# A fused attention, gated convolution and mixer kernel: four transfers placed behind the square weights, attention pieces at other places, low parts on VectorE

## The chip, the cores and the metric

The kernel runs on one core of one Trainium2 chip. The metric is the device time of one execution in microseconds (us). TensorE (PE in the rows; PEld is its weight load) multiplies, VectorE (DVE), ScalarE (ACT) and GpSimd (POOL) do the rest, and SyncE (SP; SPq is its queue) issues every transfer of the kernel. Each engine takes its instructions strictly in order, so an instruction that waits holds back all that stand behind it on its engine.

## The reference, cut to what matters

Four batches of 576 positions, 8 heads of 64. Attention is the sum of a global one on sequences averaged by 4 and a local one over a band of 7; a gated convolution layer and a mixer layer follow, each of plain float32 matmuls.

```python
def attention(q, k, v):          # (4, 8, 576, 64) each
    out_d = softmax(scale * mean4(q) @ mean4(k).T) @ mean4(v)
    out_local = softmax(where(abs(i - j) < 4, scale * q @ k.T, -1e9)) @ v
    return repeat4(out_d) + out_local

def moe(x):                      # x: (4, 576, 512)
    gate = sigmoid(causal_conv5(x, conv_w))
    return gate * (x @ w_val) @ w_out

def moe2(x):
    u = x + (relu(x.T @ w_tok1) @ w_tok2).T
    return u + relu(u @ w_ch1) @ w_ch2
```

## The kernel before

Precision is kept by splitting each float32 operand into a high part (ScalarE copies it to the type that TensorE takes (fp32r in the rows), line 718 in `hi_lo`) and a low part (the operand less its high part, line 719, on VectorE or GpSimd). Each product is then three matmuls (`mm3`, lines 284 to 286). The weights come as 64-bit words whose bits VectorE joins to float32 in three instructions (lines 153, 155, 158, `join_bits`; two fetched chunks at a time, so six instructions), then ScalarE and VectorE split them.

**Stages.** `start` (line 506) does the attention of the first batch: its order on TensorE, ScalarE, VectorE and SyncE is written out by hand in the table ORDER (line 81). In it `wf` fetches a chunk of the two square weights w_val and w_out (16 chunks, `w_fetch`, line 662), `wp` joins two chunks (`w_join`), `xf` adds the local output to `x_f` (line 637), `xh` and `xl` make the high and low part of `x_f` (lines 655 and 658), `g` and `ka` to `kd` are the taps of the convolution (lines 640 and 646). Chunks are joined in the order of the table WORD; the seventh join (`wp6`) takes chunks 9 and 11, the eighth (`wp7`) 13 and 15, all of w_out.

Then a generator `first_products` walks the four batches: `p1` (the products with w_val, called p_val; with w_out, called p_x; the token mixing r_ps and p_h) and `c1` (g_ps, the first channel product). Beside it, `mix` advances the attention of batches 1 to 3 (`attention`, line 338, cut in 26 pieces per batch by its yields) whenever the running estimate of the main stream passes the next number of the table AT (line 64). Two equal numbers let two pieces run right behind each other. Only TensorE's order is fixed by that; the other engines' instructions are put in order by a scheduler when the program is built. `c2` and `ch2_new` do the last channel product.

**Pieces of one head pair** (four per batch): `sums` (line 348; the averaged q and k on VectorE, the tile qk_d; the averaged v in two additions v_sb and vd, lines 358 and 359, on GpSimd for batches 1 and 2 and on VectorE for batch 3), `low_scores` (sc_d), `low_turn` (pt_d), `loc_scores` (sc_l), `low_out` (o_d), `loc_turn` (pt_l), `loc_out` (o_l).

**Buffers that tie the steps.** The tile for v in four parts (`load_v4`, line 300, tag v4) has one buffer (NV4 = 1): the load of a head pair's v waits until the sums of the pair before it (vd, line 359) are done. The fetched weight chunks share three buffers (NWD = 3): a fetch waits for the join of the chunk three before it. Both kinds of load stand in SyncE's one queue.

**The loads of batch 1** are put into SyncE's order behind the first batch's last v load (`begun`, line 489) for the first two head pairs; for the later two nothing holds them:

```python
if i + 1 < NHP:
    with behind(begun, i + 1):
        hpd[i + 1] = load(b, i + 1)
```

Of the kernel before, what the change touches and what calls it, by code (L numbers as in the profile page):

```python
# [46 lines left out]
MM = 0.133  # L47
FILL = {3: 1, 5: 1, 12: 1, 14: 1, 17: 1, 20: 1, 24: 1, 25: 2, 27: 1, 31: 2}
PRIME = 20, 24
# [14 lines left out]
AT = {  # L64
# [10 lines left out]
}  # L75
# [17 lines left out]
def kernel(ctx, tc, qk, vw, v4, w_val, conv_w, w_out, w_tok1, w_tok2, w_ch1, w_ch2, out):  # L93
# [40 lines left out]
    def flush():  # L134
        while pending:
            with behind_pace():
                pending.pop(0)()

    def fetch_bits(src, n, rows, shape=None):
        x = T(sb, [128, n, 2], I32, "w64", NWD, name="w64")[0:rows]  # L140
        if shape is None:
            nc.sync.dma_start(out=x, in_=src.bitcast(I32).rearrange("p (n t) -> p n t", t=2))
        else:
            nc.sync.dma_start(out=x.rearrange("p (k n) t -> p k n t", k=shape[0]),
                              in_=src.bitcast(I32).rearrange("p k (n t) -> p k n t", t=2))
        return x
# [191 lines left out]
    def attention(b):  # L338
# [9 lines left out]
        def sums(hp):  # L348
            d = hpd[hp]
            w = d.pop("v4")  # L350
            qk_d = T(sb, [128, 2, SD], F32, "qkd", ND, name="qk_d")
            qd, kd = qk_d[:, 0], qk_d[:, 1]
            qk_4 = d["qk"][:, :, 3:3 + S].rearrange("p i (a r) -> p i a r", r=4)
            nc.vector.tensor_reduce(out=qk_d, in_=qk_4, axis=AX.X, op=ALU.add)
            d["qkd"] = qd, kd
            vd = T(sb, [72, 2, 128], F32, "vd", NVD, name="vd")
            eng = nc.vector if b in (3,) else nc.gpsimd
            eng.tensor_tensor(out=w[:, 0:2], in0=w[:, 0:2], in1=w[:, 2:4], op=ALU.add)
            eng.tensor_tensor(out=vd, in0=w[:, 0], in1=w[:, 1], op=ALU.add)
            d["vd"] = [vd]  # L360
# [117 lines left out]
        for i in range(NHP + 1):  # L478
# [27 lines left out]
    def start():  # L506
# [218 lines left out]
    def hv(hs):  # L725
        return slice(hs * HS, hs * HS + HS)
# [11 lines left out]
    def p1(b):  # L738
# [88 lines left out]
        for hs in range(2):  # L827
            us.append(pair("u", "uhl", NUH))
            for c in range(KC):
# [258 lines left out]
```

## Time and profile before

| | |
|---|---|
| median of 3 runs | 615.67 us (612.16 to 616.51) |
| the profiled execution | 616.48 us; its span 614.6 us |
| busy over the span | PE 575.1 (94%), PEld 530.1 (86%), DVE 449.8 (73%), ACT 336.9 (55%), POOL 111.8 (18%) |
| GpSimd's additions and products | low parts (lines 659, 719), sums (358, 359), scaling of the exponentials (336) |
| bytes moved | 127.56 MB, mean 208 GB/s |

The 1.8 us between span and time lie outside the profile. From 225 us on TensorE is busy for 97% or more of the time; what it lacks is nearly all in the first 180 us, where the profile's slices show VectorE at nine tenths and more. So the page as a whole says "TensorE bound", and the early stages have to be read one by one.

### The profile page before, as it was taken

To read this page: it belongs to the slowest core of one execution; us is meant where nothing else is said; L and a number is where in the kernel's file an instruction comes from. 1 tells how busy PE (TensorE), PEld (TensorE's weight loads), DVE (VectorE), ACT (ScalarE), POOL (GpSimd) and SP (SyncE) were. 2 spreads that over 40 slices of the span, in tenths; PEclk is the share of its full clock that TensorE was granted. 3 is DMA by queue.
4 is the path that set the end of the run, shared out by engine and by line. 5 is a ranking of instruction groups with operands and counts; after the bars stand their busy time and mean duration, and the time that the engine had idled before them with its cause. 6 is when DMAs were issued, how large, how long until landed. Compare 5 with 4: busy or idle time off the path is not lost.

```text
span 614.6 us, 13154 instructions
## 1 busy us (share of the span) xinstructions
PE 575.1 (94%) x4975; PEld 530.1 (86%) x4975; DVE 449.8 (73%) x1019; ACT 336.9 (55%) x1118; POOL 111.8 (18%) x112
## 2 busy tenths in 40 slices
PE   8883769898999999999999999999999999999997
PEld 4772758677989889998988999999999999999997
DVE  6996987897977777762665549378975777677684
ACT  4983566566567566356635644435443645544642
POOL 1064303254102224214411410200000000000000
PEclk9877978999999999999999999999999999999999
DMA  8762144265873468794464799163977997968702
GB/s 282 243 182 88 41 137 144 67 230 190 291 245 127 144 206 261 264 307 144 144 201 149 227 309 327 34 231 142 331 259 246 351 340 236 352 212 278 260 2 77
DMA packets 84287, 127.56 MB, mean 208 GB/s; under 512 B 6720, under 2 KB 67008, under 8 KB 84224
## 3 DMA queue, kind: packets, MB, share of 16 engines
q1 hardware_dynamic: 84224, 126.72, 62.4%
q8 instruction: 39, 0.64, 0.4%
q14 instruction: 24, 0.20, 0.1%
HBM read 85.76 MB, written 40.94 MB: 206 GB/s over the span
## 4 chain that ended last, share of the span: by engine, by line
PE 61%; DVE 17%; ACT 9%; DMA 8%; issue 2%; POOL 2%; SPq 1%; DVEq 0%; ACTq 0%; POOLq 0%
PE p_o L285 6%; PE p_o L286 6%; PE p_o L284 6%; PE g_ps L284 6%; PE g_ps L285 6%; PE g_ps L286 6%; DMA qk_sb<-in_qk_dram 3%; DVE gate_sb L459 2%; PE p_x L284 2%; PE sc_l L417 2%; PE p_val L284 2%; PE p_val L285 2%; DMA v_sb<-in_v_dram 2%; PE p_val L286 2%; ACT e_l L331 2%
## 5 line engine op out<-in xcount | busy, mean ns | idle before, releaser
L284 PE MATMUL g_ps<-u_hl,w_hl 128*128 128x288 f32 x384 | 116.3, 303 | 0.3 <-ACT w_hl L168 0.3
L286 PE MATMUL g_ps<-u_hl,w_hl 128*128 128x288 f32 x384 | 113.5, 296 | 0.6 <-DVE w_hl L169 0.6
L285 PE MATMUL g_ps<-u_hl,w_hl 128*128 128x288 f32 x384 | 113.4, 295 | 0.5 <-POOL u_hl L719 0.5
L718 ACT ACTIVATE g_hl<-r_back 128x384 fp32r<-128x384 f32 x126 | 65.5, 525 | 59.5 <-PE p_o L286 53.9
L719 DVE TENSOR_TENSOR g_hl<-r_back,g_hl 128x384 fp32r<-128x384 f32 x126 | 67.7, 554 | 31.0 <-ACT g_hl L718 29.8
L285 PE MATMUL p_o<-g_hl,ch_w 128*128 128x384 f32 x252 | 85.0, 337 | 1.0 <-DVE g_hl L719 0.6
L286 PE MATMUL p_o<-g_hl,ch_w 128*128 128x384 f32 x252 | 84.7, 336 | 0.0
L284 PE MATMUL p_o<-g_hl,ch_w 128*128 128x384 f32 x252 | 84.6, 336 | 0.0
L901 ACT ACTIVATE r_sb<-g_ps 128x288 f32<-128x288 f32 x96 | 39.6, 413 | 71.7 <-PE g_ps L286 65.9
L284 PEld LDWEIGHTS g_ps<-u_hl,w_hl 128*128 128x128 f32 x384 | 72.1, 188 | 3.8 <-issue 2.1
L286 PEld LDWEIGHTS g_ps<-u_hl,w_hl 128*128 128x128 f32 x384 | 72.2, 188 | 1.2 <-DVE w_hl L169 1.2
L285 PEld LDWEIGHTS g_ps<-u_hl,w_hl 128*128 128x128 f32 x384 | 72.2, 188 | 1.0 <-POOL u_hl L719 0.8
L849 DVE TENSOR_TENSOR r_sb<-r_sb 128x288 f32<-128x288 f32 x84 | 38.2, 468 | 24.9 <-ACT r_sb L901 24.5
L284 PE MATMUL p_val<-x_hl,val_hi 128*128 128x288 f32 x128 | 41.1, 321 | 11.6 <-DVE x_f L637 10.2
L285 PEld LDWEIGHTS p_o<-g_hl,ch_w 128*128 128x128 f32 x252 | 47.3, 188 | 2.4 <-DVE g_hl L719 2.3
L284 PEld LDWEIGHTS p_o<-g_hl,ch_w 128*128 128x128 f32 x252 | 47.3, 188 | 0.0
L286 PEld LDWEIGHTS p_o<-g_hl,ch_w 128*128 128x128 f32 x252 | 47.3, 188 | 0.0
L459 DVE SCALAR_TENSOR_TENSOR gate_sb<-x_f,cw,gate_sb 128x575 f32<-128x575 f32 (+3 forms) x48 | 43.6, 908 | 0.3
L284 PE MATMUL p_x<-y_hl,out_hi 128*128 128x288 f32 x128 | 39.6, 309 | 1.0 <-ACT u_sb L770 0.9
L285 PE MATMUL p_val<-x_hl,val_hi 128*128 128x288 f32 x128 | 39.5, 308 | 0.0
L286 PE MATMUL p_x<-y_hl,out_lo 128*128 128x288 f32 x128 | 38.1, 298 | 1.3 <-DVE out_lo L674 1.3
L286 PE MATMUL p_val<-x_hl,val_lo 128*128 128x288 f32 x128 | 39.1, 306 | 0.0
(154 smaller groups left out, 1338.2 us busy)
## 6 DMA issues: line engine op xcount, KB each, us to landing
r_back<-r_dr SPq DMA_DIRECT2D x21, 1152.0 KB, 10.9
r_dr<-r_sb SPq DMA_DIRECT2D x21, 1008.0 KB, 5.6
w_hl<-w_dr SPq DMA_DIRECT2D x27, 512.0 KB, 5.8
w<-in_w_ch_dram SPq DMA_DIRECT2D x48, 256.0 KB, 3.6
qk_sb<-in_qk_dram SPq DMA_DIRECT2D x16, 589.0 KB, 3.8
w_dr<-w_hl SPq DMA_DIRECT2D x12, 512.0 KB, 3.9
v_sb<-in_vw_dram SPq DMA_DIRECT2D x16, 320.0 KB, 4.4
v_sb<-in_v_dram SPq DMA_DIRECT2D x16, 288.0 KB
```

The costliest lines, as they stand in the source:

```text
L284: nc.tensor.matmul(out_ap, lhsT=lh, rhs=rh, start=first, stop=False)
L285: nc.tensor.matmul(out_ap, lhsT=lh, rhs=rl, start=False, stop=False)
L286: nc.tensor.matmul(out_ap, lhsT=ll, rhs=rh, start=False, stop=last)
L331: nc.scalar.activation(out=e[:, o, :], in_=p[:, c, :], func=AF.Exp, scale=scale, bias=mx[:, o:o + 1], accum_out=sm[:, o:o + 1])
L417: nc.tensor.matmul(p[r0:r0 + 64, c, :], lhsT=qk[r0:r0 + 64, 0, 3 + o:3 + o + WIN], rhs=qk[r0:r0 + 64, 1, o:o + WIN], start=False, stop=(c ...
L459: nc.vector.scalar_tensor_tensor(out=g[:, sh:], in0=x[:, 0:S - sh], scalar=cw[:, hp, k:k + 1], in1=g[:, sh:], op0=ALU.mult, op1=ALU.add)
L718: nc.scalar.activation(out=hi_ap, in_=src_ap, func=AF.Copy)
L719: lo_eng.tensor_tensor(out=lo_ap, in0=src_ap, in1=hi_ap.bitcast(F32), op=ALU.subtract)
L849: nc.vector.tensor_tensor(out=r[:, o], in0=r[:, x], in1=r[:, y], op=op)
L901: paced[0] = nc.scalar.activation(out=r[:, (0, 3, 1, 2)[2 * (i % 2) + hs]], in_=p[:, 0:HS], func=AF.Relu)
```

## The change

Six edits. (1) The loads of batch 1 for its third and fourth head pair are put behind `last_sq`, the fetch of the last chunk of the square weights. (2) The loads of the second head pair keep the old rule. (3) The sums of v of batch 2 go from GpSimd to VectorE. (4) Low parts go from GpSimd to VectorE: of `x_f` for the first three head pairs of the first batch, of x in batch 3, of u in batch 1. (5) ORDER has some steps elsewhere; AT has other numbers, some of them equal. (6) One filling block of `c1` goes one place later (FILL 20 to 21).

```diff
-FILL = {3: 1, 5: 1, 12: 1, 14: 1, 17: 1, 20: 1, 24: 1, 25: 2, 27: 1, 31: 2}
+FILL = {3: 1, 5: 1, 12: 1, 14: 1, 17: 1, 21: 1, 24: 1, 25: 2, 27: 1, 31: 2}
...
-    "a1": "9.96 11.62 13.28 14.95 16.62 18.28 19.94 23.44 25.1 26.77 28.43 30.1 31.19 32.86 34.52 36.18 39.96 "
+    "a1": "9.06 11.62 13.28 14.95 16.62 18.28 21.69 21.69 25.1 26.77 28.43 30.1 31.19 32.11 34.52 36.18 39.96 "
...
-wf10 wf12 Od1 cd2 xf0 wh6 wh7 wl6 elb2 wl7 D3 Tl1 md3 xh0 g0 xl0 L3 ql2 rl2 ed3 ka0 wp4 wf14 wf9 cl1 up1 Ol1 qd3
+wf10 Od1 cd2 xf0 wh6 wf12 wh7 wl6 elb2 wl7 D3 Tl1 g0 md3 xh0 xl0 L3 ql2 rl2 ed3 ka0 wp4 wf14 wf9 cl1 up1 qd3 ml3
...
+    last_fetch = [None]
...
-            nc.sync.dma_start(out=x, in_=src.bitcast(I32).rearrange("p (n t) -> p n t", t=2))
+            last_fetch[0] = nc.sync.dma_start(out=x, in_=src.bitcast(I32).rearrange("p (n t) -> p n t", t=2))
...
-            eng = nc.vector if b in (3,) else nc.gpsimd
+            eng = nc.vector if b in (2, 3) else nc.gpsimd
...
-                with behind(begun, i + 1):
+                with behind(begun, i + 1) if i == 0 else tc.issue_after(last_sq[0].ins) if b == 1 else nullcontext():
                     hpd[i + 1] = load(b, i + 1)
...
-            last_split[0] = (nc.vector if h == NHP - 1 else nc.gpsimd).tensor_tensor(
+            last_split[0] = nc.vector.tensor_tensor(
...
             t["w", c] = fetch_bits(chunks[c][0], WB, 128)
+            last_sq[0] = last_fetch[0]
...
-                hi_lo(xf[b][k][:, hv(hs)], x[0][:, k], x[1][:, k], nc.vector if b in (1,) else nc.gpsimd)
+                hi_lo(xf[b][k][:, hv(hs)], x[0][:, k], x[1][:, k], nc.vector if b in (1, 3) else nc.gpsimd)
...
-                hi_lo(uu, us[hs][0][:, c], us[hs][1][:, c], nc.vector if b in (3,) else nc.gpsimd)
+                hi_lo(uu, us[hs][0][:, c], us[hs][1][:, c], nc.vector if b in (1, 3) else nc.gpsimd)
```

**Place A, SyncE's queue near the end of the first batch's attention.** The names w64 are chunks of the square weights (in_w_out) and then of the token weights (in_w_tok1); v4_sb_1206 is the v of batch 1's second head pair, v4_sb_1367 (1387 after) that of its third. Before:

```order
L142 DMA w64_618<-in_w_out_dram 128x512
L142 DMA w64_620<-in_w_out_dram 128x512
L303 DMA v4_sb_1206<-in_v4_dram 72x1024
L312 DMA v_sb_1213<-in_vw_dram 128x640
L303 DMA v4_sb_1367<-in_v4_dram 72x1024
L142 DMA w64_757<-in_w_out_dram 128x512
L142 DMA w64_759<-in_w_out_dram 128x512
L142 DMA w64_845<-in_w_out_dram 128x512
L142 DMA w64_946<-in_w_tok1_dram 128x512
```

After:

```order
L305 DMA v4_sb_1206<-in_v4_dram 72x1024
L144 DMA w64_618<-in_w_out_dram 128x512
L144 DMA w64_620<-in_w_out_dram 128x512
L314 DMA v_sb_1213<-in_vw_dram 128x640
L144 DMA w64_757<-in_w_out_dram 128x512
L144 DMA w64_759<-in_w_out_dram 128x512
L144 DMA w64_845<-in_w_out_dram 128x512
L144 DMA w64_946<-in_w_tok1_dram 128x512
L305 DMA v4_sb_1387<-in_v4_dram 72x1024
```

The third pair's v went from ahead of three square chunks to behind them and one token chunk; the second pair's v went from behind two square chunks to ahead of them.

**Place B, VectorE where the first batch's attention ends and p_val begins.** x_f_100 is the last of the four x_f tiles, x_hl its parts, qk_d the averaged q and k of batch 1's first head pair, y a product p_val times its gate. Before:

```order
L646 SCALAR_TENSOR_TENSOR gate_sb<-x_f_100,cw,gate_sb 128x287
L659 TENSOR_TENSOR x_hl<-x_f_100,x_hl 128x288
L646 SCALAR_TENSOR_TENSOR gate_sb<-x_f_100,cw,gate_sb 128x286
L646 SCALAR_TENSOR_TENSOR gate_sb<-x_f_99,cw,gate_sb 128x572
L646 SCALAR_TENSOR_TENSOR gate_sb<-x_f_100,cw,gate_sb 128x285
L674 TENSOR_TENSOR out_lo<-wa,out_hi 128x256
L757 TENSOR_TENSOR y_906<-p_val,gate_sb 128x288
```

After:

```order
L648 SCALAR_TENSOR_TENSOR gate_sb<-x_f_100,cw,gate_sb 128x287
L648 SCALAR_TENSOR_TENSOR gate_sb<-x_f_99,cw,gate_sb 128x572
L661 TENSOR_TENSOR x_hl<-x_f_100,x_hl 128x288
L648 SCALAR_TENSOR_TENSOR gate_sb<-x_f_100,cw,gate_sb 128x286
L356 TENSOR_REDUCE qk_d<-qk_sb 128x288
L760 TENSOR_TENSOR y_906<-p_val,gate_sb 128x288
```

The reduction qk_d now stands ahead of the first y; before, it stood behind the joins of two token chunks.

**Place C, VectorE around the maxima of the first low scores of batch 1** (mx from sc_d; w_1014 and w_1048 are token chunks). Before:

```order
L354 TENSOR_REDUCE qk_d<-qk_sb 128x288
L153 TENSOR_SCALAR wa<-w_1014 128x256
L153 TENSOR_SCALAR wa<-w_1048 64x256
L155 SCALAR_TENSOR_TENSOR wa<-w_1014,wa 128x256
L155 SCALAR_TENSOR_TENSOR wa<-w_1048,wa 64x256
L158 SCALAR_TENSOR_TENSOR wa<-w_1014,wa 128x256
L158 SCALAR_TENSOR_TENSOR wa<-w_1048,wa 64x256
L169 TENSOR_TENSOR tok_lo<-wa,tok_hi 128x256 x2
L325 TENSOR_REDUCE mx<-sc_d 72x2 x2
```

After:

```order
L327 TENSOR_REDUCE mx<-sc_d 72x2
L171 TENSOR_TENSOR tok_lo<-wa,tok_hi 128x256
L155 TENSOR_SCALAR wa<-w_1014 128x256
L327 TENSOR_REDUCE mx<-sc_d 72x2
L157 SCALAR_TENSOR_TENSOR wa<-w_1014,wa 128x256
```

Six of the weight instructions that stood ahead of the second maximum now stand behind it.

## Rows read from the trace of the kernel before

**Rows 1.** Stretches: span, then busy time (instructions) per engine, TensorE's clock, DMA share, GB/s

```profile
50.00:60.00 10.00, 1.15 (x5) 1.15 (x6) 4.54 (x9) 1.53 (x5) 3.58 (x4) 0.64 0.32 106
60.00:84.00 24.00, 18.70 (x113) 17.55 (x113) 22.09 (x52) 13.56 (x33) 5.30 (x4) 0.80 0.23 75
84.00:110.00 26.00, 21.76 (x242) 19.01 (x241) 19.03 (x51) 16.50 (x81) 7.04 (x6) 0.93 0.41 133
110.00:140.00 30.00, 27.54 (x278) 22.09 (x279) 29.37 (x60) 19.02 (x74) 12.64 (x12) 1.00 0.45 152
140.00:180.00 40.00, 36.54 (x341) 33.43 (x343) 34.79 (x86) 25.09 (x80) 8.44 (x7) 1.00 0.77 258
```

**Rows 2.** TensorE's waits: total us, times, longest us

```profile
PE p_val L284 <- DVE x_f L637: 10.2, 1, 10.2
PE sc_d L369 <- DVE qk_d L354: 3.5, 1, 3.5
PE sc_l L411 <- DVE wa L155: 1.4, 1, 1.4
PE p_x L286 <- DVE out_lo L674: 1.3, 1, 1.3
```

**Rows 3.** SyncE's queue in order of time: start us, us, what

```profile
38.26 0.33 SPq L303 DMA_DIRECT2D v_sb<-in_v_dram  x1
...
51.63 0.33 SPq L303 DMA_DIRECT2D v_sb<-in_v_dram  x1
52.01 6.44 SPq L142 DMA_DIRECT2D w<-in_w_out_dram  x3
```

**Rows 4.** GpSimd in order of time: start us, us, what, idle before and its releaser

```profile
35.77 1.26 POOL L358 TENSOR_TENSOR v_sb<-v_sb 72x512 f32<-72x512 f32 x1 [2.37 <-issue]
...
39.19 6.25 POOL L659 TENSOR_TENSOR x_hl<-x_f,x_hl 128x288 fp32r<-128x288 f32 x1 [0.96 <-ACT x_hl L656]
45.40 5.41 POOL L358 TENSOR_TENSOR v_sb<-v_sb 72x512 f32<-72x512 f32 x1
50.89 0.72 POOL L359 TENSOR_TENSOR vd<-v_sb 72x256 f32<-72x256 f32 x1
...
67.99 5.30 POOL L719 TENSOR_TENSOR x_hl<-x_f,x_hl 128x288 fp32r<-128x288 f32 x4 [10.85 <-ACT x_hl L718]
```

**Rows 5.** VectorE in order of time, 42 to 82 us

```profile
42.98 0.75 DVE L158 SCALAR_TENSOR_TENSOR wa<-w,wa 128x256 int32<-128x256 int32 x2
43.65 0.81 DVE L646 SCALAR_TENSOR_TENSOR gate_sb<-x_f,cw,gate_sb 128x575 f32<-128x575 f32 x1
...
49.41 0.28 DVE L153 TENSOR_SCALAR wa<-w 128x256 int32<-128x256 int32 x1
55.46 1.04 DVE L153 TENSOR_SCALAR wa<-w 128x256 int32<-128x256 int32 x1 [5.76 <-DMA w<-in_w_out_dram]
...
58.35 0.81 DVE L637 TENSOR_TENSOR x_f<-o_l,x_f 128x290 f32<-128x290 f32 x2
...
60.24 0.45 DVE L659 TENSOR_TENSOR x_hl<-x_f,x_hl 128x288 fp32r<-128x288 f32 x1
60.61 1.66 DVE L646 SCALAR_TENSOR_TENSOR gate_sb<-x_f,cw,gate_sb 128x286 f32<-128x286 f32 x3
...
64.25 0.46 DVE L757 TENSOR_TENSOR y<-p_val,gate_sb 128x288 f32<-128x288 f32 x1 [1.28 <-PE p_val L286]
...
71.57 1.07 DVE L646 SCALAR_TENSOR_TENSOR gate_sb<-x_f,cw,gate_sb 128x288 f32<-128x288 f32 x1
...
73.49 0.51 DVE L646 SCALAR_TENSOR_TENSOR gate_sb<-x_f,cw,gate_sb 128x288 f32<-128x288 f32 x1
...
77.35 1.34 DVE L354 TENSOR_REDUCE qk_d<-qk_sb 128x288 f32<-128x1152 f32 x1
...
81.23 0.81 DVE L325 TENSOR_REDUCE mx<-sc_d 72x2 f32<-72x288 f32 x2
```

**Rows 6.** ScalarE in order of time: the first x_f's tap

```profile
31.88 0.76 ACT L640 ACTIVATE gate_sb<-x_f,cw 128x576 f32<-128x576 f32 x1
```

**Rows 7.** VectorE's groups of one form: busy us, mean ns, idle before

```profile
L358 DVE TENSOR_TENSOR v_sb<-v_sb 72x512 f32<-72x512 f32 x4 | 3.7, 931 | 1.9 <-DMA v_sb<-in_v_dram 1.9
L359 DVE TENSOR_TENSOR vd<-v_sb 72x256 f32<-72x256 f32 x4 | 1.7, 432 | 2.6 <-PE o_d L397 2.6
```

More of the change, by code (lines that the diff above doesn't have):

```diff
@@ L81 @@
 ORDER = """
-qk0 wf0 wf1 qk1 wf2 qk2 va0 vw0 z12 S0 L0 wp0 cwf wf3 qk3 va1 vw1 D0 z14 ml0 wh1 wh0 S1 ela0 md0 wl0 ed0 wl1 S2
-elb0 D1 qd0 rd0 md1 Td0 cwj L1 ed1 ql0 wp1 wf4 wf5 va2 vw2 wf6 cd0 rl0 wh3 D2 wh2 ml1 Tl0 wl3 ela1 Od0 qd1 S3
-rd1 cl0 md2 elb1 Td1 wp2 wf7 va3 vw3 wf8 ed2 L2 ql1 wl2 rl1 cd1 qd2 up0 rd2 Ol0 wh5 ml2 wh4 wl5 ela2 wl4 Td2 wp3
-wf10 wf12 Od1 cd2 xf0 wh6 wh7 wl6 elb2 wl7 D3 Tl1 md3 xh0 g0 xl0 L3 ql2 rl2 ed3 ka0 wp4 wf14 wf9 cl1 up1 Ol1 qd3
-ml3 wh8 wh10 kb0 Od2 ela3 xf1 kc0 xh1 rd3 elb3 xl1 Tl2 kd0 z4 cl2 wl10 ql3 wl8 up2 rl3 Td3 g1 Ol2 wp5 wf11 wf13
-cd3 Od3 ka1 wh12 wh14 wl12 xf2 kb1 xh2 g2 Tl3 xl2 wl14 kc1 up3 z5 ka2 cl3 kd1 Ol3 kb2 wp6 wf15 xf3 wh11 wh9 kc2
-g3 xh3 ka3 gh xl3 kb3 kd2 kc3 wl9 kd3 na sga wl11 wp7 nb wh15 wh13 nc wl13 nd sgb wl15
+qk0 wf1 wf0 qk1 wf2 qk2 va0 vw0 z12 S0 L0 wp0 cwf wf3 qk3 va1 D0 z14 ml0 wh1 wh0 S1 ela0 md0 vw1 wl0 ed0 wl1 D1
+S2 elb0 qd0 rd0 md1 Td0 cwj L1 ed1 ql0 wp1 wf4 wf5 va2 vw2 wf6 cd0 D2 rl0 wh3 wh2 ml1 Tl0 wl3 ela1 Od0 qd1 S3
+vw3 rd1 cl0 md2 elb1 Td1 wp2 wf7 va3 wf8 ed2 L2 ql1 wl2 rl1 cd1 qd2 rd2 Ol0 up0 wh5 ml2 wh4 wl5 ela2 wl4 Td2 wp3
+wf10 Od1 cd2 xf0 wh6 wf12 wh7 wl6 elb2 wl7 D3 Tl1 g0 md3 xh0 xl0 L3 ql2 rl2 ed3 ka0 wp4 wf14 wf9 cl1 up1 qd3 ml3
+wh8 wh10 Ol1 kb0 Od2 ela3 xf1 kc0 xh1 rd3 elb3 xl1 Tl2 kd0 z4 cl2 wl10 ql3 wl8 up2 g1 rl3 Td3 Ol2 wp5 wf11 wf13
+cd3 Od3 ka1 wh12 wh14 wl12 xf2 kb1 xh2 xl2 g2 Tl3 kc1 wl14 up3 z5 ka2 cl3 kd1 Ol3 kb2 wp6 wf15 xf3 wh11 wh9 kc2
+g3 xh3 ka3 gh kd2 xl3 kb3 kc3 wl9 kd3 na sga wl11 wp7 nb wh15 wh13 nc wl13 nd sgb wl15
 """
@@ L289 @@
     xf, gate = {}, {}
-    last_gate, last_copy, last_pe, last_load, last_split = {}, [None], [None], [None], [None]
+    last_gate, last_copy, last_pe, last_load, last_split, last_sq = {}, [None], [None], [None], [None], [None]
     LU = [(0, 6), (6, 10)]
```

14 rows, old and new, of the table AT are left out of this document.

## The prediction, made before the changed kernel ran

> **What bounds the kernel now.** I read three views, in this order. The stretches first [rows 1]: from 50 to 60 us TensorE is busy 1.15 us of 10 and VectorE 4.54, so there everybody waits; from 60 to 84 us VectorE is busy 22.09 of 24 and TensorE 18.70; from 110 to 140 us VectorE has 0.63 us free, TensorE 2.46. The first 140 us are thus set by VectorE or by what VectorE waits for; later TensorE is the bound. TensorE's waits next [rows 2]: two are large, 10.2 us for x_f ahead of the first p_val and 3.5 us for qk_d ahead of the first sc_d; 1.4 and 1.3 us of the same stage follow. Then the engines in order of time, to see what x_f waited for.
>
> The 10.2 us go back like this. VectorE takes the first half of the seventh join at 49.41, then stands still for 5.76 us until a w_out chunk lands [rows 5]. That chunk is one of the three fetches that start at 52.01 [rows 3], so it landed 55.46 - 0.03 - 52.01 = 3.4 us after its issue. Its buffer had been free since the sixth join, whose first last instruction ended at about 42.98 + 0.34 = 43.3 (two take 43.65 - 42.98 = 0.67) [rows 5]. It was issued late because SyncE stood at a v load from 38.6 to 51.63 [rows 3]; and that load waited for GpSimd's vd, which ends at 50.89 + 0.72 = 51.61 [rows 4]. GpSimd was late since its low part of x_f took 6.25 us and its addition v_sb 5.41, where the same addition took 1.26 earlier [rows 4]. Both lie in a stretch in which VectorE ran without a gap; the second ends 1.1 us after VectorE's last instruction (49.41 + 0.28 = 49.69). So GpSimd got hardly anything done as long as VectorE was busy.
>
> **The change, part by part.** *SyncE's order (place A).* The chunk w64_757 no longer stands behind the third pair's v. It goes out when its buffer is free, at the sixth join. That join is later by the low parts that VectorE now makes itself: one costs 60.61 - 60.24 = 0.37 us [rows 5]. The first of them also waits, because ScalarE now makes the tap of 0.76 us [rows 6] ahead of the high part; I take 0.75 us for this one in all (bounds 0.37 and 1.13). So the sixth join is 0.75 + 0.37 = 1.1 us later, the buffer free at 44.4, the chunk there at 44.4 + 3.4 = 47.8. VectorE wants it at 49.41 + 0.20 + 0.75 + 2 x 0.37 = 51.1. The wait of 5.76 us goes, with 3.3 us to spare.
>
> From 49.41 to x_f (58.35) VectorE took 8.94 us: 5.76 waiting; the rest 3.18, of which the join's six instructions need 2 x 0.20 + 4 x 0.335 = 1.74 undisturbed, and 1.4 is disturbance by GpSimd's two instructions there (a join step took 1.04 instead of 0.28 [rows 5]). After: x_f starts at 49.41 + 1.74 + 1.49 = 52.65, which is 5.7 us earlier, and p_val with it, at about 53.15 instead of 58.85.
>
> *VectorE from there to the maxima (places B and C).* Before: 58.35 to 81.23 + 0.81 = 82.0, that is 23.65 us, with one idle time of 1.28 [rows 5]. After, the same instructions stand there but for six that moved behind the second maximum: 0.20 + 4 x 0.335 + 0.335 = 1.9 us less. qk_d (1.34 us) only changes its place, so TensorE's wait of 3.5 us goes without any work being saved. Idle I put at 0.3 instead of 1.28: qk_d and a tap of batch 0 fill the time in which p_val is made. The third pair's v now is summed in this stage instead of before it: 0.6 us of disturbance more. Four GpSimd low parts disturb as before: a tap took 1.07 instead of 0.51 beside them [rows 5], 0.56 for each, 2.3 in all [rows 4]. Sum: 23.65 - 1.9 - 1.0 + 0.6 = 21.4. The maxima end at 52.65 + 21.4 = 74.05: **8.0 us earlier**. I read the gain there and not at p_val: sc_l waits for the exponentials behind these maxima [rows 2], so TensorE, earlier still after p_x, will wait there longer than its 1.4 us.
>
> *Whether 8.0 us reach the end.* The six postponed instructions (1.9 us) have to be made later. VectorE has 26 - 19.03 = 7 us free from 84 to 110 us and 40 - 34.79 = 5.2 from 140 to 180 [rows 1]; these cover them. If that cover is gone they cost 1.9.
>
> *Low parts and sums on VectorE.* Low parts: 3 + 8 + 8 = 19, of 0.37 us each, 7.0 us; sums of batch 2: four times 0.93 + 0.43 [rows 7], 5.4 us. Together 12.4 us, of which 1.5 are in the walk above. Against it: each such GpSimd instruction held VectorE up by between 0 and 0.56 us, with 27 of them gone 0 to 15 us. I take nothing for the rest: 10.9 us are near the middle of what is saved. The bounds are 10.9 lost, and some 4 won. The 8 low parts of batch 3 stand beyond 225 us, where VectorE has room. The sums of batch 2 also wait on VectorE for transfers and for o_d, as those of batch 3 do (1.9 and 2.6 us) [rows 7]; behind a waiting one stand the next joins and y.
>
> VectorE seems too full for more work, and the Trainium skill says so too: the page Perfetto Trace Analysis, Optimizing Scalar/DVE Operations, has it that a saturated VectorE is a reason to give work to ScalarE or even GpSimd. This change does the reverse. Going by that sentence the 12.4 us would be a loss; the rows show that the work on GpSimd costs VectorE time as well, and the same section warns that moving work between those two might not help.
>
> *AT, FILL.* No instruction of TensorE is added. In batch 1 o_d and pt_l follow each other behind the first three quarters of a p_x block. I take zero, bounds 1.5 either way: that is one of the waits of TensorE left in [rows 2].
>
> **Sum.** The profiled execution: 616.48 - 8.0 = 608.5. It is 0.81 above the median of 615.67, to which I hold: 615.67 - 8.0 = **607.7 us**.
>
> **The rivals.** *The wait moves.* v4_sb_1206 now stands ahead of w64_618 and w64_620 (place A) and waits for GpSimd's first vd. If GpSimd is shut out there as it was from 39.19 on (6.25 + 5.41 instead of 1.26 and about 1), chunk 618 goes out at about 42.4, lands at 45.8, and VectorE, at its join at about 43, waits 3 us. Gain 5.0: 610.7. Against it: v4_sb_1038, which feeds that sum, stands two chunks earlier in the queue, and the sum at 35.77 ran freely.
>
> *VectorE gives part of it back.* From 110 to 180 us it has 0.63 + 5.2 = 5.8 us free [rows 1]. Work of 1.9, of 5.4 and, to 250 us, of 8 x 0.37 = 3.0 comes, 10.3 in all; if no disturbance is saved, 4.5 us are on the path: 612.2.
>
> *More is gained.* TensorE's granted clock is 0.64 from 50 to 60 us, 0.80 to 84 us and 0.93 to 110 us [rows 1], so 7.2, 9.6 and 3.6 us at its lower level, each time about a wait. If the stretch that goes with the wait for qk_d (half of the 9.6) is at the upper level, TensorE does the work of 4.8 us in 2.4, and where it is the bound the gain is 10.4; with 1.5 from the pieces' new places 11.9: 603.8.
>
> *Slower.* VectorE saturated from 60 to 250 us, every added instruction on the path: 615.67 - 5.7 + 12.4 = 622.4. It decides when disturbance saves less than about 6 us and VectorE's free time cannot be used because TensorE's fixed order makes it wait at other times. The rule on saturated engines above would have it so. Against it: 7 + 5.2 us free [rows 1].
>
> *Nothing happens:* chunk 757 is late for another reason (its join or the DMA engines), 615.7. Against it: the free buffer at 43.3 and a DMA share of 0.32 [rows 1].
>
> **The numbers.** Forecast 0.56 (604.5 to 611), more gained 0.18, moved wait 0.09, given back 0.08, nothing 0.04, slower 0.05. A measurement of this kernel can tell about 1% from no change, 6.2 us, so below 609.5 is faster, above 621.8 slower. Four fifths of the forecast lie below 609.5, with all of "more": 0.63 faster, 0.05 slower, 0.32 within. The range reaches from 602, beyond "more gained", to 613.5, beyond "given back"; it leaves out "nothing", "slower" and a tenth at the edges. Its lower end is what would come if both large waits went in full, 615.67 - 13.7.
>
> **What would show it.** VectorE has no wait for a w_out chunk at the seventh join; p_val begins at 52.5 to 54.5 us; no wait of sc_d for qk_d; the first maxima end at 73 to 76; sc_l waits longer than before, for ScalarE's exponentials. SyncE does not stand for GpSimd between 38 and 52 us. At 225 us the lead is still 8 us. Wrong: VectorE waits for w64_618 at about 43 us; the lead at 140 us is 8 and at 250 us 4; or v_sb and vd of batch 2 show waits on VectorE that TensorE then has too.

## The result, and the profile after

The changed kernel takes 609.25 us (median of 10 runs, 606.22 to 612.17), beside 614.48 us for the kernel before (10 runs, 611.38 to 617.54): a ratio of 0.990, with a 95% interval from 0.987 to 0.993. The ratio is reckoned from the single executions; the medians alone give 0.9915, a gain of 5.2 us instead of about 6. Forecast were 607.7 us, from 602.0 to 613.5, a gain of 8.0 reckoned from 615.67. The profiled execution took 612.17 us, with a span of 610.4 us; that of before 616.48, with 614.6. Executions of one kernel spread by half a per cent either way, so a difference of 2 or 3 us between two profiles is no finding by itself. Line numbers of the changed kernel are 2 or 3 higher than those of before.

The stretches after, in the columns of [rows 1]:

```profile
50.00:60.00 10.00, 8.05 (x78) 5.64 (x74) 10.00 (x20) 6.05 (x14) 0.00 (x0) 0.83 0.26 84
60.00:84.00 24.00, 18.49 (x149) 16.38 (x148) 23.05 (x58) 13.88 (x45) 5.78 (x6) 0.93 0.31 100
84.00:110.00 26.00, 23.35 (x211) 19.72 (x210) 18.46 (x47) 14.45 (x67) 5.87 (x5) 0.87 0.37 111
110.00:140.00 30.00, 27.43 (x282) 22.34 (x282) 28.73 (x60) 19.83 (x82) 13.04 (x12) 1.00 0.56 188
140.00:180.00 40.00, 38.23 (x383) 35.55 (x382) 35.43 (x87) 27.30 (x97) 2.44 (x2) 1.00 0.76 250
```

From 50 to 60 us VectorE no longer stands still, and TensorE is busy 8.05 us instead of 1.15. In the last stretch TensorE is busy 38.23 us of 40 instead of 36.54. From 84 to 110 us it is busy longer than before (23.35 us against 21.76) with fewer matmuls (211 against 242), at a granted clock of 0.87 instead of 0.93.

TensorE's waits after, as in [rows 2] (the four largest, and the one for x_f):

```profile
PE sc_l L413 <- ACT e_d L333: 6.0, 4, 3.0
PE pt_d L593 <- ACT pts_l L609: 3.3, 1, 3.3
PE p_x L287 <- DVE y_hl L722: 2.3, 1, 2.3
PE sc_d L537 <- DVE x_f L639: 1.8, 1, 1.8
...
PE p_val L286 <- DVE x_f L639: 1.0, 1, 1.0
```

The wait of p_val for x_f is down from 10.2 us to 1.0, that of 3.5 us for qk_d is gone; sc_l waits longer, and p_x and pt_d wait where they did not.

SyncE's queue, GpSimd and VectorE after, in order of time (start us, us, what), as in [rows 3 to 5]:

```profile
46.79 8.21 SPq L144 DMA_DIRECT2D w<-in_w_out_dram  x3
55.10 0.37 SPq L144 DMA_DIRECT2D w<-in_w_tok_dram  x1
55.57 0.35 SPq L305 DMA_DIRECT2D v_sb<-in_v_dram  x1
```

```profile
38.77 1.27 POOL L360 TENSOR_TENSOR v_sb<-v_sb 72x512 f32<-72x512 f32 x1 [3.29 <-DMA v_sb<-in_v_dram]
40.12 1.12 POOL L361 TENSOR_TENSOR vd<-v_sb 72x256 f32<-72x256 f32 x1
```

```profile
28.96 0.29 DVE L155 TENSOR_SCALAR wa<-w 128x256 int32<-128x256 int32 x1 [0.96 <-DMA w<-in_w_val_dram]
...
33.50 1.41 DVE L661 TENSOR_TENSOR x_hl<-x_f,x_hl 128x288 fp32r<-128x288 f32 x1 [0.77 <-ACT x_hl L658]
...
45.28 0.48 DVE L155 TENSOR_SCALAR wa<-w 128x256 int32<-128x256 int32 x2
...
53.16 0.48 DVE L155 TENSOR_SCALAR wa<-w 128x256 int32<-128x256 int32 x2
...
54.90 0.81 DVE L639 TENSOR_TENSOR x_f<-o_l,x_f 128x290 f32<-128x290 f32 x2
...
75.50 0.45 DVE L327 TENSOR_REDUCE mx<-sc_d 72x2 f32<-72x288 f32 x1
```

The seventh join (53.16) runs without a wait, its w_out chunks having been issued from 46.79 on. The addition that took 5.41 us takes 1.27, and vd ends at 41.24 instead of 51.61. The second maximum ends at 75.50 + 0.45 = 75.95 instead of 82.0.

### The profile page after: what moved, and what is told of

It reads as the page before. It is cut to its first block, busy times and chain, and to the rows that moved or that the text cites. A ratio compares the mean times of both kernels' runs of the same rounds, so it can differ in the third digit from the quotient of the medians.

```text
span 610.4 us, 13163 instructions
## 1 busy us (share of the span) xinstructions
PE 578.0 (95%) x4975; PEld 530.7 (87%) x4975; DVE 454.4 (74%) x1046; ACT 336.5 (55%) x1118; POOL 73.5 (12%) x85
## 4 chain that ended last, share of the span: by engine, by line
PE 58%; DVE 21%; DMA 10%; ACT 9%; issue 2%; POOL 0%; SPq 0%; ACTq 0%; DVEq 0%; POOLq 0%
PE p_o L287 6%; PE p_o L288 6%; PE p_o L286 6%; PE g_ps L286 6%; PE g_ps L287 5%; PE g_ps L288 5%; DMA w<-in_w_ch_dram 2%; DVE gate_sb L648 2%; PE p_x L286 2%; PE sc_l L419 2%; DVE gate_sb L461 2%; ACT e_l L333 2%; DMA w<-in_w_val_dram 2%; DVE wa L157 2%; DMA qk_sb<-in_qk_dram 2%; PE p_val L286 2%
## 5 line engine op out<-in xcount | busy, mean ns | idle before, releaser
L461 DVE SCALAR_TENSOR_TENSOR gate_sb<-x_f,cw,gate_sb 128x575 f32<-128x575 f32 (+3 forms) x48 | 40.9, 852 | 0.2
L287 PE MATMUL p_x<-y_hl,out_hi 128*128 128x288 f32 x128 | 38.0, 297 | 2.3 <-DVE y_hl L722 2.3
L286 PE MATMUL p_x<-y_hl,out_hi 128*128 128x288 f32 x128 | 39.3, 307 | 0.5
```

Of the source, the lines that this page charges most:

```text
L286: nc.tensor.matmul(out_ap, lhsT=lh, rhs=rh, start=first, stop=False)
L287: nc.tensor.matmul(out_ap, lhsT=lh, rhs=rl, start=False, stop=False)
L461: nc.vector.scalar_tensor_tensor(out=g[:, sh:], in0=x[:, 0:S - sh], scalar=cw[:, hp, k:k + 1], in1=g[:, sh:], op0=ALU.mult, op1=ALU.add)
```

## The experiments

The table has each kernel's median, the median of before that it stands against, and the ratio with its 95% interval. A ratio of 0.990 is about 6 us. Distances from the changed kernel are reckoned from 0.990; by the medians (0.9915) each gap to a slower kernel is 0.9 us smaller.

| kernel | us | before | ratio |
|---|---|---|---|
| changed kernel | 609.25 | 614.48 | 0.990 (0.987 to 0.993) |
| before + hold of the third pair's v load | 613.34 | 614.91 | 0.9968 (0.9941 to 0.9996) |
| before + first batch's low parts on VectorE | 615.23 | 614.91 | 1.0004 (0.9973 to 1.0036) |
| before + new list | 614.19 | 615.37 | 0.9993 (0.9964 to 1.0023) |
| before + sums of batch 2 on VectorE + AT, FILL | 612.53 | 615.63 | 0.9957 (0.9929 to 0.9985) |
| changed − hold | 610.92 | 614.91 | 0.9934 (0.9904 to 0.9964) |
| changed − first batch's low parts | 611.16 | 614.91 | 0.9938 (0.9906 to 0.9970) |
| changed − new list | 610.83 | 615.37 | 0.9928 (0.9899 to 0.9957) |
| changed − AT, FILL | 612.04 | 615.37 | 0.9952 (0.9923 to 0.9981) |
| changed − sums of batch 2 | 613.06 | 615.56 | 0.9962 (0.9935 to 0.9989) |
| changed − sums of batch 2, x of batch 3, u of batch 1 | 614.59 | 615.37 | 0.9988 (0.9963 to 1.0012) |
| changed + two repairs of the list | 608.45 | 615.56 | 0.9896 (0.9852 to 0.9940) |
| changed + x and u of batch 0 on VectorE | 617.19 | 615.56 | 1.0023 (0.9994 to 1.0052) |

### The wait at the seventh join

Theory 1 is the prediction's: the v load's place in SyncE's queue is the cause of the wait. Theory 2: GpSimd is the cause, which gets nothing done beside VectorE; with the low parts taken off it the load would be free in time, and the hold is not needed. Each was tried alone and taken out of the changed kernel.

The hold alone, on the kernel before (with the bookkeeping of last_sq that it needs):

```diff
-                with behind(begun, i + 1):
+                with behind(begun, i + 1) if i == 0 else tc.issue_after(last_sq[0].ins) if b == 1 else nullcontext():
                     hpd[i + 1] = load(b, i + 1)
```

> The kernel before with one part of the change: the v load of the third pair is held until the last square-weight fetch has been issued, so that it stands behind the three w_out fetches of the seventh join in SyncE's queue. Low parts, order list, times and sums stay those of before. Theory 1 (the queue position of the v load is the cause): the wait of 5.76 us at the seventh join goes, p_val begins 5 to 6 us earlier, the time is about 609. Theory 2 (the cause is GpSimd, which gets nothing done while VectorE is busy): the wait goes too, but the third low part of x_f, which p_val needs, still stands on GpSimd behind its 5.4 us addition; p_val is earlier by 0 to 3 us only, the time 612 to 615.

The wait is gone (seventh join at 51.41 without a gap) and p_val begins at 53.66 instead of 58.85. The time falls by 0.3%, about 2 us (interval 0.2 to 3.6). So p_val does what Theory 1 says, and the time does not: it lies where Theory 2 had it, for another reason than Theory 2 gave.

The low parts alone, on the kernel before:

```diff
-            last_split[0] = (nc.vector if h == NHP - 1 else nc.gpsimd).tensor_tensor(
+            last_split[0] = nc.vector.tensor_tensor(
```

> The kernel before with one part of the change: the first two low parts of x_f of the first batch are made on VectorE instead of GpSimd, as the third was already or now is too; the v load of the third pair stays ahead of the w_out fetches in SyncE's queue. Theory 1: the v load still waits for GpSimd's vd, and the fetches behind it with it; VectorE's wait at the seventh join stays over 3 us and the gain is under 2 us, so 613 or more. Theory 2: GpSimd, free of the low parts, ends vd at about 41 to 43 us instead of 51.6, the v load no longer stands in the way, and the wait goes without any change to the queue: about 609.

The wait shrinks to 0.41 us, p_val begins at 55.24, and the time stays (1.0004). Theory 2 is right about the wait; again nothing reaches the end.

The changed kernel without the hold, and with the first batch's low parts back on GpSimd (the two diffs above, reversed; the edit moves three low parts, not two as the expectations have it):

> The changed kernel without the hold: the v load of the third pair goes back to its old place ahead of the three w_out fetches of the seventh join; all else as changed. Theory 1: SyncE stands at that load again, the seventh join waits, 4 to 6 us are lost against the changed kernel: 613 to 615. Theory 2: in the changed kernel vd of the second pair ends at 41.24 us, so that the load would stand at most until then, while the buffer of the fetch behind it comes free only at 46.8: the hold is worth nothing, 609 within 1.

> The changed kernel with the first two low parts of x_f of the first batch back on GpSimd; the hold and all else as changed. Theory 1: since the fetches no longer stand behind the v load, the wait at the seventh join does not come back, and the time is 609 to 611. Theory 2: GpSimd is shut out again while VectorE is busy (an instruction of about 1 us takes 5 to 6), x_f's low parts come late and p_val, which needs them, with them: 2 to 5 us lost, 611 to 614.

In neither does the seventh join wait (53.25 and 53.52, no gap). They come out 0.34% and 0.38% above the changed kernel, some 2 us each, which the intervals don't separate from nothing. The wait of Theory 1 does not come back, as Theory 2 said; the low parts may be worth the 2 us of Theory 2's lower end.

### The list, and what the wait is worth

Since both single parts took the wait away and gained 0 to 2 us, the rest had to carry the 6 us. First the list:

```diff
 ORDER = """
-(list of before)
+(list of after)
```

> The kernel before with one part of the change: the new ORDER list for the first stage (first batch) and nothing else: no hold, low parts and sums on GpSimd, the old times AT and FILL. The two single parts tried before took the wait at the seventh join away (5.76 us before, 0.0 with the hold alone, 0.5 with the low parts alone), and p_val began 5.2 and 3.6 us earlier, yet the time fell by 1.6 us and not at all. Theory 3: most of what the change gains comes from the new list (fewer and shorter waits of TensorE between 60 and 100 us, since qk_d and two taps no longer stand ahead of the maxima): 610 to 611. Theory 1 and 2 (the removed wait): the list alone gives nothing, 614 to 615.

> The changed kernel with the ORDER list of before; hold, low parts, sums, AT and FILL as changed. The counterpart of the run with the new list alone. Theory 3 (the list carries it): 612 to 614, about as with the hold alone. Theory 1 and 2 (the wait carries it, with both parts together): 609 to 610.

The new list alone gives nothing measurable (0.9993); without it the changed kernel still gains 0.72%. Theory 3 falls. The profile with the list alone shows something else. Here the v load stands ahead of the w_out chunks and GpSimd makes the low parts, both as before. GpSimd and VectorE there, in order of time:

```profile
38.09 1.86 POOL L358 TENSOR_TENSOR v_sb<-v_sb 72x512 f32<-72x512 f32 x1 [2.35 <-DMA v_sb<-in_v_dram]
40.03 1.12 POOL L359 TENSOR_TENSOR vd<-v_sb 72x256 f32<-72x256 f32 x1
41.11 0.79 POOL L659 TENSOR_TENSOR x_hl<-x_f,x_hl 128x288 fp32r<-128x288 f32 x1
```

```profile
52.98 0.49 DVE L153 TENSOR_SCALAR wa<-w 128x256 int32<-128x256 int32 x2
```

No wait at the seventh join, although neither was changed; the list only puts GpSimd's second low part behind vd, where before it stood ahead of the addition. The wait of 5.76 us [rows 5] came with two GpSimd instructions shut out one after the other, 6.25 and 5.41 us [rows 4]; that pair stands in the profile of before and in none of the 13 others.

### Low parts, sums and times

What was left were the edits that the prediction priced at nothing. All later moves undone, then the sums alone (the first of the three places):

```diff
-            eng = nc.vector if b in (2, 3) else nc.gpsimd
+            eng = nc.vector if b in (3,) else nc.gpsimd
...
-                hi_lo(xf[b][k][:, hv(hs)], x[0][:, k], x[1][:, k], nc.vector if b in (1, 3) else nc.gpsimd)
+                hi_lo(xf[b][k][:, hv(hs)], x[0][:, k], x[1][:, k], nc.vector if b in (1,) else nc.gpsimd)
...
-                hi_lo(uu, us[hs][0][:, c], us[hs][1][:, c], nc.vector if b in (1, 3) else nc.gpsimd)
+                hi_lo(uu, us[hs][0][:, c], us[hs][1][:, c], nc.vector if b in (3,) else nc.gpsimd)
```

> The changed kernel with the later low parts and sums back on GpSimd: sums of batch 2, low parts of x of batch 3, low parts of u of batch 1. The prediction took these 10.9 us of VectorE work as worth nothing: 609 within 1.5. If the work costs VectorE time on the path, the time falls to 605 to 607; if GpSimd's disturbance was the greater, it rises to 611 to 613, and then part of the gain between 110 and 165 us (5.3 us of lead at 165 us against 3.5 at 127) comes from here.

> The changed kernel with one thing back on GpSimd: the sums of batch 2 (v_sb and vd); all low parts stay on VectorE. Undoing all three later moves cost 5.3 us. Theory 4: the sums do it, since between 131 and 200 us TensorE's gaps were 1.1 to 1.7 us in every run with these sums on VectorE and the new times, and 4.5 to 5.5 in every run without one of the two; so 613 to 614.5, TensorE busy 54 to 56 us of the 60 from 140 to 200 us (58.2 in the changed kernel), gaps of about 5 us from 131 to 200. Rival: the low parts of x and u do it, which stand beyond 225 us; then 609 to 610 and TensorE busy 58.

Without the later moves nearly the whole gain is gone (0.9988), hold, list and first low parts notwithstanding. The sums are most of it: 0.9962, some 3.8 us above the changed kernel. The further 1.6 us for the low parts of x and u are within the intervals.

What the sums do is seen from 126 to 139 us. GpSimd and VectorE with the sums on GpSimd (changed kernel without them):

```profile
129.42 1.79 POOL L360 TENSOR_TENSOR v_sb<-v_sb 72x512 f32<-72x512 f32 x1
131.17 2.35 POOL L722 TENSOR_TENSOR u_hl<-u_sb,u_hl 128x288 fp32r<-128x288 f32 x3
```

```profile
130.35 0.44 DVE L327 TENSOR_REDUCE mx<-sc_d 72x2 f32<-72x288 f32 x1
130.72 2.15 DVE L155 TENSOR_SCALAR wa<-w 128x256 int32<-128x256 int32 x1
...
136.39 0.85 DVE L327 TENSOR_REDUCE mx<-sc_l 128x6 f32<-128x384 f32 x2
```

The same place with the sums on VectorE (changed kernel):

```profile
132.77 0.44 DVE L327 TENSOR_REDUCE mx<-sc_d 72x2 f32<-72x288 f32 x1
133.13 0.28 DVE L155 TENSOR_SCALAR wa<-w 128x256 int32<-128x256 int32 x1
...
136.93 0.85 DVE L327 TENSOR_REDUCE mx<-sc_l 128x6 f32<-128x384 f32 x2
137.71 1.07 DVE L360 TENSOR_TENSOR v_sb<-v_sb 72x512 f32<-72x512 f32 x1
138.89 0.42 DVE L361 TENSOR_TENSOR vd<-v_sb 72x256 f32<-72x256 f32 x1
```

A join step takes 2.15 us instead of 0.28 while GpSimd makes the addition and two low parts, so the maxima of sc_l start 6.04 us after that of sc_d instead of 4.16: 1.9 us later. This is no chance of one execution: the step takes 2.15 to 2.17 us in all six profiles with these sums on GpSimd, that of before among them, and 0.27 to 0.28 in all eight with them on VectorE. On VectorE these two sums come behind the maxima, in a stretch in which it waits for qk with or without them (2.41 us and 3.04 us), so they cost nothing there. TensorE's largest waits from 131 to 200 us, of the kernel before, of the changed one without the sums, and of the changed one:

```profile
PE pt_l L431 <- ACT x_f L402: 1.3, 1, 1.3
PE p_val L284 <- DVE y L757: 0.9, 1, 0.9
```

```profile
PE sc_l L413 <- ACT e_d L333: 2.0, 1, 2.0
PE g_ps L288 <- DVE w_hl L171: 1.3, 2, 0.9
PE pt_l L433 <- ACT x_f L404: 1.3, 1, 1.3
PE p_val L286 <- DVE y L760: 0.9, 1, 0.9
```

```profile
PE sc_l L413 <- ACT e_d L333: 1.0, 1, 1.0
PE g_ps L288 <- DVE w_hl L171: 0.7, 2, 0.4
```

Only pt_l's wait (139.83 us) follows at once on the late maxima. Without the sums g_ps, p_val and sc_l wait at 153 to 175 us; how that hangs on the sums was not followed.

Then the times AT and FILL of before in the changed kernel (FILL's 21 back to 20, and six of AT's lists, one of which is shown):

```diff
-FILL = {3: 1, 5: 1, 12: 1, 14: 1, 17: 1, 21: 1, 24: 1, 25: 2, 27: 1, 31: 2}
+FILL = {3: 1, 5: 1, 12: 1, 14: 1, 17: 1, 20: 1, 24: 1, 25: 2, 27: 1, 31: 2}
...
-    "ch2": "224.02 229.26 235.49 242.51 248.93 254.65 266.56 272.02 284.95 289.47 295.12 299.35",
+    "ch2": "228.79 234.73 240.68 246.62 253.05 258.51 269.89 275.83 287.6 291.92 297.31 301.64",
```

> The changed kernel with the times AT and the FILL of before, so that TensorE's filling pieces stand in their old places; all else as changed. The prediction took them as worth nothing, within 1.5: 609 within 1.5. If the new places carry part of the gain (the lead grows from 3.5 us at 127 us to 5.3 at 165 us, where a wait of 1.28 us of pt_l at 145 us is gone), 611 to 612.

0.9952, some 3 us lost. In the same stretch the waits of pt_l and p_val stay away, but sc_l waits three times:

```profile
PE sc_l L413 <- ACT e_d L333: 3.9, 3, 1.7
```

The second sc_l comes at 184.81 us there, behind one block each of x_ps and p_val; in the changed kernel two of each stand ahead of it, and it waits for nothing. So the pieces' places fill a wait that the sums alone leave. The two together, on the kernel before:

```diff
-            eng = nc.vector if b in (3,) else nc.gpsimd
+            eng = nc.vector if b in (2, 3) else nc.gpsimd
...
-FILL and AT of before
+FILL and AT of after
```

> The kernel before with two parts of the change: the sums of batch 2 on VectorE, and the new times AT and FILL. No hold, no moved low part, the old ORDER list; so VectorE still waits for the w_out chunk at the seventh join (5.8 us) and p_val begins at about 58 to 59 us. Theory 4: these two parts together are what reaches the end: TensorE's gaps from 131 to 200 us fall from 4.5 to between 1 and 2 us, TensorE is busy 58 to 59 us of the 60 from 140 to 200 us, and the time is 611 to 612, 3 to 4 us under before. Rival: the two only pay if TensorE comes 4 to 7 us earlier into this stretch, as it does in the changed kernel (transfers then start earlier too); then 614 to 615.

0.9957: 2.6 us (interval 0.9 to 4.4), a little under what was expected, without hold, list or any low part. TensorE is busy 59.06 us of the 60 from 140 to 200 us, and what it waits for from 131 to 200 us is:

```profile
PE g_ps L286 <- DVE w_hl L169: 0.5, 1, 0.5
PE sc_l L411 <- ACT e_d L331: 0.3, 1, 0.3
```

One expectation failed: this kernel should have waited 5.8 us at the seventh join, as it has there the order and the low parts of before. It did not:

```profile
39.50 2.17 POOL L659 TENSOR_TENSOR x_hl<-x_f,x_hl 128x288 fp32r<-128x288 f32 x1 [1.08 <-ACT x_hl L656]
42.90 1.32 POOL L358 TENSOR_TENSOR v_sb<-v_sb 72x512 f32<-72x512 f32 x1 [1.23 <-DMA v_sb<-in_v_dram]
```

```profile
53.28 0.48 DVE L153 TENSOR_SCALAR wa<-w 128x256 int32<-128x256 int32 x2
```

Up to 58 us VectorE, ScalarE, GpSimd and SyncE take the same instructions in the same order in this profile and in that of before; so the wait of 5.76 us does not follow from the order, it differs from execution to execution. And so the rival, that the two parts only pay with an early start, is not settled: p_val began at 55.52 instead of 58.85, and the third block of p_h 3.2 us earlier than before, nearly the 3.5 of the changed kernel.

The other profiles can be read the same way. Call lead how much earlier the same work starts than in the profile of before. From the third block of p_h (127 to 135 us) to the end the lead grows by 0.7 to 3.6 us in the six profiles that have the sums of batch 2 on VectorE and the new times (the run with 12 more low parts, below, left aside). It shrinks by 2.7 to 3.9 in the three that have one of the two. With neither it shrinks by 1.2 and 1.3 (the hold, the low parts alone) or stays (the list alone).

### Two attempts to go further

Two places of the list repaired, at which p_val lost time against the forecast (vw3 behind va3, and xh0 ahead of g0):

```diff
-vw3 rd1 cl0 md2 elb1 Td1 wp2 wf7 va3 wf8 ed2 L2 ql1 wl2 rl1 cd1 qd2 rd2 Ol0 up0 wh5 ml2 wh4 wl5 ela2 wl4 Td2 wp3
-wf10 Od1 cd2 xf0 wh6 wf12 wh7 wl6 elb2 wl7 D3 Tl1 g0 md3 xh0 xl0 L3 ql2 rl2 ed3 ka0 wp4 wf14 wf9 cl1 up1 qd3 ml3
+rd1 cl0 md2 elb1 Td1 wp2 wf7 va3 vw3 wf8 ed2 L2 ql1 wl2 rl1 cd1 qd2 rd2 Ol0 up0 wh5 ml2 wh4 wl5 ela2 wl4 Td2 wp3
+wf10 Od1 cd2 xf0 wh6 wf12 wh7 wl6 elb2 wl7 D3 Tl1 md3 xh0 g0 xl0 L3 ql2 rl2 ed3 ka0 wp4 wf14 wf9 cl1 up1 qd3 ml3
```

> The changed kernel with two places of its list altered, where p_val lost 2.2 us against the forecast: the third pair's w_val load is issued later, so that the next batch's qk load no longer stands ahead of the chunk w64_416 for which VectorE waited 0.96 us at 28.96; and ScalarE makes the high part of the first x_f ahead of the tap, for which the low part waited 0.77 us. If these are the loss, p_val begins at 53 to 54 us instead of 55.4. If an early start of p_val reaches the end, 607 to 608; if, as in the runs with the hold alone and the list alone, it is lost again by 135 us (waits of TensorE and its lower clock between 60 and 100 us), 609 to 610.

0.9896 over 6 runs, not to be told from the changed kernel. The sixth join is 0.8 us earlier (44.52), but the seventh is not (53.23), and p_val begins at 55.48: GpSimd's addition now runs from 44.40 to 48.55 beside VectorE and takes the 0.8 us back. (A tap and a low part on VectorE at 48 to 50 us take 1.09 and 0.98 us there, 0.80 and 0.44 in the changed kernel.) Both waits are gone, but that did not bring p_val forward.

Twelve more low parts on VectorE:

```diff
-... x[1][:, k], nc.vector if b in (1, 3) else nc.gpsimd)
+... x[1][:, k], nc.vector if b in (0, 1, 3) else nc.gpsimd)
...
-... us[hs][1][:, c], nc.vector if b in (1, 3) else nc.gpsimd)
+... us[hs][1][:, c], nc.vector if b in (0, 1, 3) else nc.gpsimd)
```

> The changed kernel with the low parts of x and of u of batch 0 on VectorE too, 12 more of 0.37 us (4.5 us), eight of them between 126 and 136 us, where GpSimd makes them now beside a VectorE that is busy 14.2 of 15 us. If a low part on GpSimd holds VectorE up by as much as it costs there (0.56 us measured beside a tap), the time falls by 1 to 2 us: 607 to 608. If VectorE's fullness decides, it rises by 2 to 4: 611 to 613.

It loses all and more: 1.0023, some 7.5 us above the changed kernel, for work of 12 x 0.37 = 4.5 us. TensorE's two largest waits from 60 to 200 us:

```profile
PE sc_l L413 <- ACT e_d L333: 8.0, 3, 6.5
PE p_val L287 <- DVE x_hl L722: 4.6, 2, 3.2
```

The four low parts of x come ahead of the first maxima, which end at 79.32 instead of 75.95; and at 163.8 and 167.7 us p_val waits for low parts that VectorE makes only after joins and taps. No version tried is measurably faster than the changed kernel.

## Why the prediction was right, and where it was not

The time was forecast well: 607.7, measured 609.25, inside the range. The reasons hold only in part. Errors of opposite sign cancelled, on the early edits and on the later ones, and the kernel before came out 1.2 us under the 615.67 from which the forecast was reckoned; that the number is so close is luck.

**SyncE's order.** Right as a mechanism: no wait at the seventh join, SyncE does not stand for GpSimd between 38 and 52 us. The size was wrong. p_val begins at 55.41, 3.4 us earlier and not 5.7: VectorE waited 0.96 us for a w_val chunk at 28.96, and the first low part cost 0.77 of waiting and 1.41, so that the sixth join came at 45.28, 3.4 us later than before, where 1.1 were forecast.

**VectorE to the maxima.** The stretch was right: from x_f to the end of the maxima 21.05 us (75.95 - 54.90), forecast 21.4. The maxima are 6.1 us earlier, and not 8.0, as x_f starts at 54.90 and not at 52.65. qk_d's wait is gone, and sc_l waits 3.0 us instead of 1.4, as foreseen.

**"Whether 8.0 us reach the end".** This step failed. The first batch's fifth and eighth y, before and after:

```profile
84.18 0.46 DVE L757 TENSOR_TENSOR y<-p_val,gate_sb 128x288 f32<-128x288 f32 x1 [0.68 <-PE p_val L286]
...
101.13 0.46 DVE L757 TENSOR_TENSOR y<-p_val,gate_sb 128x288 f32<-128x288 f32 x1
```

```profile
76.20 0.45 DVE L760 TENSOR_TENSOR y<-p_val,gate_sb 128x288 f32<-128x288 f32 x1
...
97.39 0.46 DVE L760 TENSOR_TENSOR y<-p_val,gate_sb 128x288 f32<-128x288 f32 x1 [0.61 <-PE p_val L288]
```

The lead in the profiled pair is 6.5 us at sc_l (79.01 against 85.53), 8.0 at the fifth y and 3.7 at the eighth; it is 3.5 at the third block of p_h (131.74 against 135.27), rises to 5.8 at 184 us and is 4.2 at the end. At 225 us, where 8 were to be left, it is between 5 and 6. The runs say it more sharply: the hold alone removes the wait and gains 2 us, the low parts alone or the list alone nothing, and the changed kernel without the later moves, with all that was to bring the 8.0 us, gains 0.7 us. (This last one keeps the new times, which without the sums lose again: in its profile a lead of 3.8 us at the third p_h is gone at the end. The early edits together, without the later ones and the times, were not run.) Two things stand behind it. The 5.76 us of waiting came from one profile; in 13 others, four of which keep the v load ahead of the chunks, it is 0.41 us or less, and one of them has the same instructions in the same order up to there. How often the kernel before has it in executions without a profile is not known. And part of what is won seems lost to the clock. Between the fifth and the eighth y of the changed kernel the granted clock falls (last section); in the two profiles in which it stayed at 1.00 from 80 to 96 us, that of the two repairs and that of the old times, 8.0 and 7.3 us are still there at the third p_h. With the hold alone the lead of 5.2 us at p_val is 1.4 there, and the granted clock from 84 to 110 us is 0.82 where before had 0.93.

**"I take nothing for the rest" (low parts and sums).** This step failed too, the other way: the later moves are worth 5.4 us (0.9988 - 0.990; about 3 to 8 by the two intervals), 3.8 of them the sums (about 1 to 6). The bounds were 10.9 lost to 4 won, and the zero did not follow from them: the middle of 0 to 15 us saved is 7.5 and not 10.9, so 3.4 us lost should have stood in the sum. The price of a disturbance was taken from low parts, 0.56 us each; one join step beside an addition paid 1.9 us, at a place on which the next maxima hang. And the cost on VectorE, 5.4 us, was counted in full, although the first pair's sums stand in a wait for qk.

**AT, FILL.** Taken as zero with bounds of 1.5; taking them back costs 3.2 us (about 1 to 6 by the two intervals). What was missed is that they close waits of sc_l at 170 to 190 us; the profile of before shows only 0.4 us there (179.64).

**The rivals.** "The wait moves" did not come (the sixth join runs without a gap at 45.28), nor did "VectorE gives part of it back" and "Slower"; but the run with 12 more low parts shows where the last would begin. "More is gained" is seen in one execution: the profiled one of the two repairs, at a granted clock of 1.00 from 54 to 110 us, took 604.85 us, near the 603.8 of that rival; the medians show that it is not the rule. VectorE was also less full than was said ahead: before, it is busy 153.5 of the first 180 us, and its slices there show six to nine tenths. The Trainium skill, Perfetto Trace Analysis, Optimizing Scalar/DVE Operations, speaks for giving a saturated VectorE's work away and doubts that moving it between VectorE and GpSimd helps; here the move to VectorE gains 3.8 us for the sums of batch 2 and loses 7.5 for the low parts of batch 0.

The parts don't add up: 2.0, 0 and 0.4 for hold, low parts and list alone, 2.6 for sums and times, make 5.0 of the 6.1 (5.2 by the medians), with intervals of about 1.8 us each. The largest single share that the runs show is that of the sums with the new times; neither of these two was put into the kernel before by itself. The rest, some 2.4 us by the single runs and 3.5 by difference, is not resolved part by part.

## What to carry to other kernels

A long wait in one profile may be that execution's own, as here, where the same instructions in the same order once waited 5.76 us and once not at all: before its removal is booked as gain, look whether it follows from the order of the program or from two engines meeting by chance, and ask a second profile. Price an instruction on GpSimd by what stands on VectorE beside it and by who waits for that, not by a mean: moving an operation to the fuller engine pays where it falls into that engine's waits, and costs more than its duration where it stands ahead of something that TensorE waits for. An early lead is worth something only if no later wait and no fall of the clock eats it; read the lead at several places, not at the one where it is largest.

## What the runs showed of the hardware

**The clock can outweigh the edits.** From 54 to 80 us the profiles of the changed kernel and of the one with two repairs, which differ only in the list, are alike: p_x's second block begins at 73.39 and 73.30, and both have a wait of 3.0 us ahead of sc_l at 79.0. The stretches from 54 to 80 and 80 to 96 us, of the changed kernel, then of the repaired one:

```profile
54.00:80.00 26.00, 18.54 (x169) 16.25 (x161) 25.77 (x62) 16.49 (x44) 4.64 (x5) 1.00 0.29 91
80.00:96.00 16.00, 13.96 (x118) 12.05 (x113) 12.86 (x33) 9.02 (x43) 3.63 (x3) 0.68 0.32 98
```

```profile
54.00:80.00 26.00, 18.37 (x165) 16.14 (x153) 25.77 (x63) 16.49 (x44) 4.65 (x5) 1.00 0.30 91
80.00:96.00 16.00, 13.45 (x147) 11.71 (x145) 15.92 (x45) 12.08 (x64) 3.77 (x3) 1.00 0.51 158
```

After the same wait the granted clock fell to its lower level (1.2 GHz) in one execution (118 matmuls in the 16 us) and stayed at the upper (2.4 GHz) in the other (147). The fifth y starts at 76.20 and 76.13, the eighth at 97.39 and 93.42, and the third block of p_h begins at 131.74 and at 127.28: 4.5 us, as much as any part of the change, 4.0 of them by the eighth y. Why it fell in the one and not in the other is not shown.

**VectorE and GpSimd shut each other out for more than one instruction.** The Trainium skill, SBUF — State Buffer, Who interferes with whom, says that of two instructions that need the shared ports the first keeps them to its end and the other stands still. The join step that took 2.15 us instead of 0.28 fits with standing still, though a duration alone does not tell that from slowing down. But, other than the Trainium skill has it there, it did not get its turn when the addition ended (129.42 + 1.79 = 131.21); it ended at 132.87, when two low parts more were done. In the changed kernel the same step runs in 0.28 us in the middle of six low parts on GpSimd. It went the other way in the profile of before, where GpSimd's low part of 0.8 us took 6.25 [rows 4]. What decides which engine goes first was not tried, and the same order of instructions went both ways (6.25 us in the profile of before, 2.17 in that of before with sums and times).
